# Retention and two MLPs on one core: the first in-projection of blocks 2 and 3 made wholly of seven block products

## The chip, the cores and the metric

The kernel runs on one core of a Trainium2 chip. The metric is the time of one execution on the device, in microseconds; of several runs the median is taken. A profile is one further execution, recorded instruction by instruction.

## What is computed

Three layers follow one another on 3072 tokens (4 batches of 768), all in float32:

```python
for t in range(S):                       # 8 heads of 64
    state = gamma * state + einsum('bhd,bhe->bhde', k[:, :, t], v[:, :, t])
    y[:, :, t] = scale * einsum('bhd,bhde->bhe', q[:, :, t], state)
x = y as (3072, 512)

h = np.maximum(x @ w_in, 0.0)            # w_in 512 x 2048
x = h * h @ w_out                        # w_out 2048 x 512

xn = x / sqrt(mean(x * x) + 1e-6) * rms_g
g = xn @ w_gate                          # 512 x 1536
out = (g * sigmoid(g) * (xn @ w_val)) @ w_out
```

The change is in the first product of the first MLP, `x @ w_in`.

## The kernel before, in words

**Precision.** TensorE multiplies numbers that were split in two: a high part (a cast to `fp32r`, on ScalarE) and a low part (value minus high part, on VectorE, line 102). One product of two float32 matrices is three matmuls: high x high, high x low, low x high (`mm3`, lines 281 to 283; `proj`, line 323). So every operand, weight or activation, costs a cast on ScalarE and a subtraction on VectorE before TensorE can read it. `split` does both.

**Tiling.** Tokens are cut into six blocks of 512. The first MLP's hidden width of 2048 is cut into 16 slices f of 128. Blocks 0 and 1 go through `block1`, slice by slice: 12 matmuls of `proj` make a slice of `x @ w_in`, `act1` squares it on ScalarE and casts the high half of s, VectorE makes the low half, and `out1` (12 matmuls, called by `tail1`) adds the slice's part of the second product, one slice behind. The low half of s is read first by the second matmul of `out1`.

Blocks 2 and 3 are taken as a pair, and so are 4 and 5. For a pair the in-projection can be done in four groups n of four slices, each by seven block products in place of eight (`in_pair`): the weights of a group are made into seven *in-units* (P1 to P7, sums and differences of quarters), the activations of the pair into seven operands `X[P1]` to `X[P7]`, and each of the seven products is 2 halves m x 2 halves c x 3 = 12 matmuls of 128x512. The second product of the pair is done in the same way from *out-units* (class `Out`). Units are stored in HBM as they are made (`made_units`, five steps M1 to M5 of one or two VectorE operations of 128x512 each, ahead of them one or two steps that gather rows, `whole_rows`), and are fetched through a ring of seven slots of 512 KB, from which every product takes one; `unit_done` then asks for the one seven products on.

For the first group of blocks 2 and 3 the kernel before does not use seven products. `in_phase` does slices 0 to 3 classically: 4 slices x 2 blocks x `proj`, 96 matmuls. Groups 1 to 3 use `in_pair`.

**Other work that is woven in.** The retention is computed in chunks of 128 tokens; each *visit* is some hundred small matmuls, a mask on VectorE (lines 985 and 990), a state update, and the loads of later chunks' queries, keys and values. A query must land and be decayed on GpSimd (line 944) before the next visit's scores (line 967) can use it. In block 1 there is a visit behind the projection of every even slice; in the pair's phase there are two per group, behind P6 and P3. `tick` converts one 128-row slice of a later layer's weights. `first_x` makes the operands X of blocks 2 and 3 from their retention outputs, in steps.

**Order.** The program's order is written out by hand, and each engine and each DMA queue keeps it. Python generators are advanced at fixed places by `next(...)`: `made` (out-units), `made_in` (in-units), `coming_xs` (`first_x`). In `block1` the order in a slice f is: `early(f)`, background work, projection, `act1` on ScalarE, `late(f)`, the visit with its mask if f is even, VectorE's low half of s, the visit's follow-up, `last_of(f)`, and `tail1`, which is `out1(f - 1)`. `out1(15)` itself is issued in the next phase, behind that phase's first 12 matmuls. For block 1 the hooks are `early1`, `late1` and `last1`.

Of the kernel before, what the change touches and what calls it, by code (L numbers as in the profile page):

```python
# [1 line left out]

# [47 lines left out]
NCL = 2  # L50
RING_AT = 13
# [9 lines left out]
def retention_then_two_mlps(  # L61
# [63 lines left out]
    W = {}  # L125
# [325 lines left out]
    def in_phase(xs, w_of, after, between):  # L451
        for f in range(2 * NCL):
            q, r, i = f // 4, f % 4 // 2, f % 2
            w = w_of(f)
            for t in range(2):
                proj(w, xs[t], ph[t])
                between(f, t)
                if i == 0:
                    act[r][t][q] = slot(f"act{r}{t}")
                a = act[r][t][q][:, i, :]  # L460
                nc.scalar.activation(a, ph[t], AF.Relu)
                nc.scalar.activation(a, a, AF.Square)
                after(f, t)

# [141 lines left out]
    def first_x(raws, xs):  # L606
        y = {(h, t): raws[t].t[:, 2 * h:2 * h + 2, :] for h in range(2) for t in range(2)}

        def put(src, wide=False):
            if wide:  # L610
                t = big("xop", F32R)
                o = [t[:, 0:2], t[:, 2:4]]
            else:
                o = [slot("xop", F32R) for _ in range(2)]
            split(*o, src, nc.vector)
            return o

        yield
        X[P1] = put(y[0, 0])
        yield  # L620
        X[P2] = put(y[1, 0])
        yield
        other = put(y[0, 1])
        X[P3] = put(y[1, 1])
        for a in ((X[P1], X[P2]), (other, X[P3])):
            xs.append([[a[k // 2][n][:, k % 2, :] for k in range(KC)] for n in range(2)])
        yield
        sub(y[0, 0], y[0, 1], y[0, 0])
        yield
        sub(y[0, 1], y[1, 1], y[0, 1])  # L630
        yield
        sub(y[1, 1], y[1, 1], y[0, 0])
        yield
        X[P6] = put(y[1, 1])
        yield
        X[P5] = put(y[0, 0])
        yield
        sub(y[1, 0], y[1, 0], y[1, 1])
        yield
        X[P7] = put(y[0, 1], True)  # L640
        yield
        X[P4] = put(y[1, 0], True)
        yield
# [242 lines left out]
    with tc.manual_schedule():  # L886
# [432 lines left out]
        def in_units():  # L1319
            for q in (1, 2, 3, 0):  # L1320
                yield from whole_rows("i", q)
                spare = cf.tile([128, 512], F32, tag="f", name="sm")
                for n, _ in enumerate(made_units(ui, q, row_tiles.pop(("i", q)), lambda: spare, True)):
                    if n == 1:
                        request("i", q + 1)
                    yield

        xs, raws1 = [], []
# [3 lines left out]
        def sink1(c):  # L1332
            nonlocal coming_xs
            t = c // B - 2
            if t == len(raws1):
                raws1.append(Raw())
                if t:
                    coming_xs = first_x(raws1, xs)
                    next(coming_xs)
            return raws1[t]  # L1340

        def early1(f):
            if f % 2:
                next(made, None)

        def late1(f):
# [4 lines left out]
            if f % 2:  # L1351
                next(made, None)
# [5 lines left out]

        stream += [ui[q][k] for q in range(NCL // 2, NQ) for k in IN_ORDER]

        def last1(f):
# [3 lines left out]
            next(made, None)  # L1365
# [4 lines left out]
            if f >= 4:  # L1370
                next(made_in, None)
            if f in (10, 12, 14):
                next(coming_xs)

        block1(1, cur, sink1, (0, 2, 4, 6, 8, 10, 12, 14), early1, late1, last1)
        for _ in made:
            pass
        stores()

# [25 lines left out]
        def between1(f, t):  # L1405
            if f == 0 and t == 0:
                tail1()
            else:
                background()
            mask()  # L1410

# [6 lines left out]
        def after1(f, t):  # L1418
            if t == 0:
                stores()  # L1420
                if f:
                    tick(ahead=False)
                if f and f % 2 == 0:
                    next_chunk()
            elif f % 2:
                kv, _ = visit(at_chunk, pa, True)
                after_visit(at_chunk, sink2(at_chunk), kv)
            if t or f > 1:
                next(coming_xs, None)
            if f % 2 == 0 or t == 0:  # L1430
                next(made_in, None)
            if (t or f) and len(ring) < 7:
                more_ring()

        def after1b(n, k):
            background()
            mask()
            stores()
            at_step = k in (P2, P5, P4) or k == P1 and NCL // 2 < n < NQ - 1
            if at_step:  # L1440
                tick(ahead=False)
            if (n, k) == (NCL // 2, P1) or k == P5 or k == P4 and n < NQ - 1:
                next_chunk()
# [3 lines left out]
            if at_step:  # L1447
                next(made_in, None)
            if n == NCL // 2 and k in (P2, P6, P5):
                next(coming_xs, None)  # L1450
# [16 lines left out]
        for _ in made_in:  # L1467
# [309 lines left out]
```

## Time and profile before

| | us |
|---|---|
| median of 3 runs | 1083.77 |
| lowest and highest run | 1083.15, 1086.19 |
| the profiled execution | 1085.07 |
| its span, first to last instruction | 1083.3 |

The span is what the trace covers; the execution's own time is 1.8 us longer. TensorE is called PE in the rows, its weight loads PEld, VectorE DVE, ScalarE ACT, GpSimd POOL, SyncE's queue of DMA issues SPq. L102 is line 102 of the kernel. Times in rows are microseconds from the span's start. In this execution block 1 ends, and the phase of blocks 2 and 3 begins, at 229 us; the classical first quarter lasts to 259.3 us.

### The profile page before, as it was taken

What the parts mean: (1) busy time and instruction counts of PE and PEld (TensorE: products, weight loads), DVE (VectorE), ACT (ScalarE), POOL (GpSimd) and SP (SyncE); (2) the same over time, 40 slices, a digit from 0 to 9 for tenths busy, and PEclk for the clock granted to TensorE, in tenths of its full rate; (3) what the DMA queues carried; (4) which work ended last, traced back from release to release, by engine and by line L of the source; (5) the groups of instructions that cost most, each with busy time, mean ns of one, the idle gap of its engine ahead of it and who ended that gap; (6) DMA issues with size and microseconds to landing.
All of it is one profiled execution on the core that took longest, in us unless ns stands there. A gap on an engine that the chain in (4) does not pass through costs nothing. (4 is left out here: it accounts for less than half of the span.)

```text
span 1083.3 us, 16663 instructions
## 1 busy us (share of the span) xinstructions
PE 1077.3 (99%) x6269; PEld 886.5 (82%) x6269; DVE 785.9 (73%) x1073; ACT 592.9 (55%) x915; POOL 77.2 (7%) x65
## 2 busy tenths in 40 slices
PE   9999999999999999999999999999999999999998
PEld 7788888888888887888888887888888888888887
DVE  6888689978757995579788887994343896433585
ACT  5766445767777658885465555453333554233442
POOL 3000142315210000000000000000000000000000
PEclk9999999999999999999999999999999999999999
DMA  9979889999999979987569979767567667555563
GB/s 361 337 240 353 268 283 359 380 366 357 366 367 339 344 267 394 366 279 241 199 229 338 375 274 380 256 208 241 194 231 250 193 213 251 193 194 193 194 214 117
DMA packets 109172, 303.49 MB, mean 280 GB/s; under 512 B 11124, under 2 KB 34444, under 8 KB 109092
## 3 DMA queue, kind: packets, MB, share of 16 engines
q1 hardware_dynamic: 108912, 302.18, 78.6%
q8 instruction: 50, 0.82, 0.3%
q10 hardware_dynamic: 180, 0.24, 0.1%
q14 instruction: 30, 0.25, 0.1%
HBM read 213.76 MB, written 88.62 MB: 279 GB/s over the span
## 5 line engine op out<-in xcount | busy, mean ns | idle before, releaser
L502 ACT CAST o<-act 128x1024 fp32r<-128x1024 f32 x101 | 105.5, 1051 | 110.0 <-DVE act L109 50.2
L102 DVE TENSOR_TENSOR o<-act,o 128x1024 fp32r<-128x1024 f32 x101 | 123.0, 1223 | 26.6 <-ACT o L502 26.5
L282 PE MATMUL ph<-o,ring 128*128 128x512 f32 x228 | 88.8, 389 | 0.0
L283 PE MATMUL ph<-o,ring 128*128 128x512 f32 x228 | 88.6, 388 | 0.0
L281 PE MATMUL ph<-o,ring 128*128 128x512 f32 x228 | 88.5, 388 | 0.0
L281 PE MATMUL pb<-xop,ring 128*128 128x512 f32 x208 | 81.3, 391 | 0.0
L323 PE MATMUL ph<-xh,w_i 128*128 128x512 f32 x248 | 81.1, 390 | 0.0
L283 PE MATMUL pb<-xop,ring 128*128 128x512 f32 x208 | 80.9, 389 | 0.0
L282 PE MATMUL pb<-xop,ring 128*128 128x512 f32 x208 | 80.9, 389 | 0.0
L281 PE MATMUL pa<-xop,ring 128*128 128x512 f32 x200 | 78.3, 391 | 0.3 <-ACT act L116 0.3
L109 DVE TENSOR_TENSOR act<-act 128x1024 f32<-128x1024 f32 x64 | 78.2, 1222 | 0.3
L283 PE MATMUL pa<-xop,ring 128*128 128x512 f32 x200 | 77.8, 389 | 0.0
L282 PE MATMUL pa<-xop,ring 128*128 128x512 f32 x200 | 77.8, 389 | 0.0
L281 PE MATMUL ph<-xop,ring 128*128 128x512 f32 x192 | 75.3, 392 | 0.8 <-ACT part L116 0.6
L283 PE MATMUL ph<-xop,ring 128*128 128x512 f32 x192 | 74.7, 389 | 0.0
L282 PE MATMUL ph<-xop,ring 128*128 128x512 f32 x192 | 74.7, 389 | 0.0
L112 DVE TENSOR_TENSOR part<-pr,part 128x512 f32<-128x512 f32 x38 | 25.7, 690 | 52.5 <-ACT part L116 51.2
L780 ACT ACTIVATE t<-part 128x512 f32<-128x512 f32 x54 | 34.1, 632 | 49.5 <-DVE part L112 49.5
L116 ACT COPY part<-ph 128x512 f32<-128x512 f32 x52 | 29.7, 587 | 52.3 <-PE ph L283 52.3
L323 PEld LDWEIGHTS ph<-xh,w_i 128*128 128x128 f32 x248 | 46.5, 188 | 10.2 <-ACT w_o L136 0.4
L282 PEld LDWEIGHTS ph<-o,ring 128*128 128x128 f32 x228 | 42.8, 188 | 9.7 <-DVE o L102 0.9
L281 PEld LDWEIGHTS ph<-o,ring 128*128 128x128 f32 x228 | 42.8, 188 | 9.0
(256 smaller groups left out, 2625.2 us busy)
## 6 DMA issues: line engine op xcount, KB each, us to landing
ring<-wu SPq DMA_DIRECT2D x84, 512.0 KB, 4.3
ring<-up SPq DMA_DIRECT2D x63, 512.0 KB, 4.3
ring<-uo SPq DMA_DIRECT2D x56, 512.0 KB, 4.4
ring<-ui SPq DMA_DIRECT2D x49, 512.0 KB, 7.6
wu<-ring SPq DMA_DIRECT2D x42, 512.0 KB, 6.8
raw<-w1i SPq DMA_DIRECT2D x16, 512.0 KB, 6.9
raw<-w1o SPq DMA_DIRECT2D x16, 512.0 KB, 7.0
vkt<-vk SPq DMA_DIRECT2D x16, 512.0 KB, 7.0
```

Source lines behind the costliest of these rows:

```text
L102: eng.tensor_tensor(out=dst_l, in0=src, in1=dst_h.bitcast(F32), op=ALU.subtract)
L109: eng.tensor_tensor(out=out_, in0=a, in1=b, op=ALU.subtract)
L112: eng.tensor_tensor(out=out_, in0=a, in1=b, op=ALU.add)
L116: nc.scalar.copy(dst[:, m], acc[m])
L281: nc.tensor.matmul(acc, ah, bh, start=start, stop=False, **more)
L282: nc.tensor.matmul(acc, ah, bl, start=False, stop=False, **more)
L283: nc.tensor.matmul(acc, al, bh, start=False, stop=stop, **more)
L323: nc.tensor.matmul(h, w[:, a, k * 128:(k + 1) * 128], x[b][k], start=n == 0, stop=n == len(order) - 1)
L502: nc.scalar.copy(h, src)
L780: nc.scalar.activation(t, g, AF.Silu)
```

## The change

All four groups of the in-projection of blocks 2 and 3 are done by `in_pair`; `in_phase` and its hooks are gone. For that the in-units of group 0 are needed at the start of the phase and not for blocks 4 and 5 only, so `in_units` goes through the groups in the order 0, 1, 2, 3, begins two slices earlier in block 1 and is advanced more often there; the out-units are advanced less often in block 1, and what is left of them (`making_1`) follows in the phase of blocks 2 and 3. The ring is filled from slice 10 on (`RING_AT`) and not from 13. `first_x` makes no second set of plain operands (`other`) any more, and has three differences and the operand P6 ready by the end of block 1; P5, P7 and P4 follow behind the first three products of group 0.

```diff
-NCL = 2
-RING_AT = 13
+RING_AT = 10
...
-    def first_x(raws, xs):
+    def first_x(raws):
...
-        other = put(y[0, 1])
-        X[P3] = put(y[1, 1])
-        for a in ((X[P1], X[P2]), (other, X[P3])):
-            xs.append([[a[k // 2][n][:, k % 2, :] for k in range(KC)] for n in range(2)])
+        put(P3, y[1, 1])
         yield
         sub(y[0, 0], y[0, 1], y[0, 0])
-        yield
         sub(y[0, 1], y[1, 1], y[0, 1])
         yield
         sub(y[1, 1], y[1, 1], y[0, 0])
         yield
-        X[P6] = put(y[1, 1])
-        yield
-        X[P5] = put(y[0, 0])
+        put(P6, y[1, 1])
+        yield
+        put(P5, y[0, 0])
+        yield
+        put(P7, y[0, 1], True)
         yield
         sub(y[1, 0], y[1, 0], y[1, 1])
...
-            for q in (1, 2, 3, 0):
+            for q in range(NQ):
                 yield from whole_rows("i", q)
...
         def early1(f):
-            if f % 2:
-                next(made, None)
+            if f % 2 and f != 11:
+                next(made)
+            if f == NF1 - 1:
+                next(coming_xs)
 
         def late1(f):
...
-            if f % 2:
-                next(made, None)
+            if f == NF1 - 1:
+                next(coming_xs)
+            if f % 2 and f > 1:
+                next(made_in)
+            elif f % 2:
+                next(made)
...
-        stream += [ui[q][k] for q in range(NCL // 2, NQ) for k in IN_ORDER]
+        stream += [ui[q][k] for q in range(NQ) for k in IN_ORDER]
 
         def last1(f):
             stores()
             if f >= RING_AT:
                 more_ring()
-            next(made, None)
+            if f < 8 or f % 2 == 0 and f != 10:
+                next(made)
             if f == MORE_AT:
                 more_steps(W2_SOON)
             if f > MORE_AT and f % 2:
                 tick(ahead=False)
-            if f >= 4:
+            if f >= 2:
                 next(made_in, None)
-            if f in (10, 12, 14):
+            if f in (8, 10, 14, 15):
                 next(coming_xs)
...
-        for _ in made:
-            pass
         stores()
+        making_1 = chain(made_in, made)
...
+        def after1(n, k):
+            if (n, k) == (0, P1):
+                tail1()
+            else:
+                background()
             mask()
             stores()
-            at_step = k in (P2, P5, P4) or k == P1 and NCL // 2 < n < NQ - 1
+            at_step = k in (P2, P5, P4) or k == P1 and 0 < n < NQ - 1
             if at_step:
                 tick(ahead=False)
-            if (n, k) == (NCL // 2, P1) or k == P5 or k == P4 and n < NQ - 1:
+            if k == P5 or k == P4 and n < NQ - 1:
                 next_chunk()
             if k in (P6, P3):
                 kv, _ = visit(at_chunk, (ph, pb)[(n + 1) % 2] if k == P6 else pa, True)
                 after_visit(at_chunk, sink2(at_chunk), kv)
             if at_step:
-                next(made_in, None)
-            if n == NCL // 2 and k in (P2, P6, P5):
-                next(coming_xs, None)
+                next(making_1, None)
+            if n == 0 and k in (P1, P2, P6):
+                next(coming_xs)
+            if (n, k) == (0, P1):
+                more_ring()
...
-        in_phase(xs, lambda f: W[("i", f)], after1, between1)
-        for n in range(NCL // 2, NQ):
-            in_pair(n, after1b)
+        for n in range(NQ):
+            in_pair(n, after1)
```

## Rows read from the trace of the kernel before

**Rows 1.** The page's totals: busy us, share of the span, instructions

```profile
PE 1077.3 (99%) x6269; PEld 886.5 (82%) x6269; DVE 785.9 (73%) x1073; ACT 592.9 (55%) x915; POOL 77.2 (7%) x65
```

**Rows 2.** TensorE's waits: who for whom, us in total, times, longest

```profile
PE pr L1095 <- DVE st L1080: 1.3, 1, 1.3
PE ph L281 <- ACT part L116: 0.6, 2, 0.4
PE pa L281 <- ACT act L116: 0.3, 1, 0.3
```

**Rows 3.** Line 323 from 229 us on: duration ns min/median/max, first and last start

```profile
L323 PE MATMUL ph<-xop,w_i x96: 388/389/499, 229.0 to 256.3; 128*128 128x512 f32 x96
```

**Rows 4.** Timeline of TensorE across block 1's end: start us, duration, instruction

```profile
229.02 2.88 PE L323 MATMUL ph<-xop,w_i 128*128 128x512 f32 x12
231.74 0.39 PE L281 MATMUL pa<-s,w_o 128*128 128x512 f32 x1
231.97 0.39 PE L282 MATMUL pa<-s,w_o 128*128 128x512 f32 x1
```

**Rows 5.** Timeline of VectorE, slices 14 and 15; in brackets idle time and releaser

```profile
220.87 0.43 DVE L985 TENSOR_TENSOR causal<-ph,seen_sb 128x256 f32<-128x256 f32 x1 [1.04 <-PE ph L967]
...
223.84 0.69 DVE L109 TENSOR_TENSOR sm<-sm,rows 128x512 f32<-128x512 f32 x1
224.44 1.10 DVE L102 TENSOR_TENSOR made<-rows,made 128x512 fp32r<-128x512 f32 x1
225.47 3.20 DVE L102 TENSOR_TENSOR xop<-raw,xop 128x1024 fp32r<-128x1024 f32 x2
228.59 1.78 DVE L102 TENSOR_TENSOR s<-r,s 128x512 fp32r<-128x512 f32 x1
230.29 0.68 DVE L102 TENSOR_TENSOR wps<-rows,wps 128x512 fp32r<-128x512 f32 x1
```

**Rows 6.** Timeline of VectorE in slice 13

```profile
214.75 1.22 DVE L102 TENSOR_TENSOR xop<-raw,xop 128x1024 fp32r<-128x1024 f32 x1
215.89 0.68 DVE L102 TENSOR_TENSOR made<-rows,made 128x512 fp32r<-128x512 f32 x1
```

**Rows 7.** Timeline of GpSimd beside rows 5

```profile
224.07 0.93 POOL L1033 TENSOR_TENSOR st<-st,sdec_sb 128x256 f32<-128x256 f32 x1 [9.79 <-DMA rows<-rows_i]
224.96 1.49 POOL L955 TENSOR_TENSOR vkt<-vkt,vdec_sb 128x512 f32<-128x512 f32 x1
227.91 1.91 POOL L944 TENSOR_TENSOR qnt<-qnt,qdec_sb 128x512 f32<-128x512 f32 x1 [1.46 <-DMA qnt<-qT]
```

**Rows 8.** Timeline of ScalarE, the cast of slice 15's s

```profile
227.80 0.62 ACT L339 CAST s<-r 128x512 fp32r<-128x512 f32 x1
```

**Rows 9.** Windows of two stretches (classical quarter, group 1): length, busy us (instructions), clock, DMA

```profile
229.00:259.30 30.30, 30.30 (x269) 25.04 (x267) 20.61 (x27) 21.18 (x36) 9.02 (x6) 1.00 1.00 396
259.30:282.20 22.90, 22.90 (x249) 18.68 (x241) 19.54 (x34) 15.18 (x26) 9.37 (x7) 1.00 1.00 369
```

**Rows 10.** Line 1357, the ring's first seven loads, 512 KB each

```profile
DMA to landing us min/median/max: 8.5/8.8/9.6
```

**Rows 11.** Timeline of TensorE: visits of the classical quarter, then scores of group 1's two

```profile
242.71 0.69 PE L1002 MATMUL pr<-vkt 128*64 128x64 f32 x16
...
245.47 11.18 PE L323 MATMUL ph<-xop,w_i 128*128 128x512 f32 x48
256.58 0.69 PE L1002 MATMUL pr<-vkt 128*64 128x64 f32 x16
...
270.21 0.85 PE L967 MATMUL ph<-qnt,kTt 64*64 64x128 f32 x32
...
281.37 0.85 PE L967 MATMUL pa<-qnt,kTt 64*64 64x128 f32 x32
```

**Rows 12.** Timeline of SyncE's queue: issue of the query load between these two

```profile
270.51 0.33 SPq L922 DMA_DIRECT2D qnt<-qT  x1
```

**Rows 13.** Timeline of GpSimd: decay of that query

```profile
278.06 1.30 POOL L944 TENSOR_TENSOR qnt<-qnt,qdec_sb 128x512 f32<-128x512 f32 x1 [3.79 <-DMA qnt<-qT]
```

More of the change, by code (lines that the diff above doesn't have):

```diff
@@ L1 @@
 from contextlib import ExitStack
+from itertools import chain
 import numpy as np
@@ L449, in unit_done @@
         load_unit(ring_at[0] + 6)
[L451 to L463, printed above, removed]
     class Out:
@@ L604, in raw_x, with put @@
         yield
-    def first_x(raws, xs):
+    def first_x(raws):
         y = {(h, t): raws[t].t[:, 2 * h:2 * h + 2, :] for h in range(2) for t in range(2)}
-        def put(src, wide=False):
+        def put(k, src, wide=False):
             if wide:
                 t = big("xop", F32R)
-                o = [t[:, 0:2], t[:, 2:4]]
+                X[k] = [t[:, 0:2], t[:, 2:4]]
             else:
-                o = [slot("xop", F32R) for _ in range(2)]
-            split(*o, src, nc.vector)
-            return o
+                X[k] = [slot("xop", F32R) for _ in range(2)]
+            split(*X[k], src, nc.vector)
         yield
-        X[P1] = put(y[0, 0])
+        put(P1, y[0, 0])
         yield
-        X[P2] = put(y[1, 0])
+        put(P2, y[1, 0])
         yield
-        other = put(y[0, 1])
-        X[P3] = put(y[1, 1])
-        for a in ((X[P1], X[P2]), (other, X[P3])):
-            xs.append([[a[k // 2][n][:, k % 2, :] for k in range(KC)] for n in range(2)])
+        put(P3, y[1, 1])
         yield
         sub(y[0, 0], y[0, 1], y[0, 0])
-        yield
         sub(y[0, 1], y[1, 1], y[0, 1])
@@ L633, in first_x @@
         yield
-        X[P6] = put(y[1, 1])
+        put(P6, y[1, 1])
         yield
-        X[P5] = put(y[0, 0])
+        put(P5, y[0, 0])
+        yield
+        put(P7, y[0, 1], True)
         yield
         sub(y[1, 0], y[1, 0], y[1, 1])
-        yield
-        X[P7] = put(y[0, 1], True)
-        yield
-        X[P4] = put(y[1, 0], True)
+        put(P4, y[1, 0], True)
         yield
@@ L1326, in in_units @@
                     yield
-        xs, raws1 = [], []
+        raws1 = []
         made_in = in_units()
@@ L1337, in sink1 @@
                 if t:
-                    coming_xs = first_x(raws1, xs)
+                    coming_xs = first_x(raws1)
                     next(coming_xs)
@@ L1403, in retention_then_two_mlps @@
         stream += [uo[q][k] for k, q in out_1.seq]
[L1405 to L1410, printed above, removed]
         def next_chunk():
@@ L1416, in next_chunk @@
             at_chunk += 1
[L1418 to L1428, printed above, removed]
-                next(coming_xs, None)
-            if f % 2 == 0 or t == 0:
-                next(made_in, None)
[L1432 to L1436, printed above, removed]
+        def after1(n, k):
[3 more added lines that the diff above has]
+                background()
             mask()
             stores()
-            at_step = k in (P2, P5, P4) or k == P1 and NCL // 2 < n < NQ - 1
+            at_step = k in (P2, P5, P4) or k == P1 and 0 < n < NQ - 1
             if at_step:
                 tick(ahead=False)
-            if (n, k) == (NCL // 2, P1) or k == P5 or k == P4 and n < NQ - 1:
+            if k == P5 or k == P4 and n < NQ - 1:
                 next_chunk()
@@ L1447, in after1b @@
             if at_step:
-                next(made_in, None)
-            if n == NCL // 2 and k in (P2, P6, P5):
-                next(coming_xs, None)
+                next(making_1, None)
[3 more added lines that the diff above has]
+                more_ring()
             if n == NQ - 1 and k in (P2, P6, P3):
@@ L1465, in retention_then_two_mlps @@
             background()
-        for _ in made_in:
+        for _ in making_1:
             pass
```

## The prediction

> **What bounds the kernel now.** I read the page's totals first, then TensorE's waits, then the stretch that the change rewrites, engine by engine. TensorE is busy for 99% of the span [rows 1], and its waits on other engines come to 2.2 us in the whole execution [rows 2]; the same view of 100 to 340 us alone lists none. Busy time of pipelined matmuls proves little, so I looked at their starts: twelve matmuls of the classical product take from 229.02 to 231.74 us [rows 4], 0.227 us for each, and the matmuls of the seven-product groups have the same form. So TensorE is packed: a matmul left out is worth 0.227 us, and any wait that is made for it costs its full length. What decides is whether VectorE, ScalarE, GpSimd and the DMAs, all busy in this stretch [rows 9], still deliver in time after the work has been laid out anew.
>
> **What is removed and added on TensorE.** The classical first quarter is 8 projections of 12 matmuls, the 96 of [rows 3]. The new group 0 is 7 products of 2 x 2 x 3 = 84. So 12 matmuls go: 12 x 0.227 = **-2.72 us**. Both layouts have the same eight visits of the retention, so the small matmuls and the switches between them and the large ones cancel. No other large matmul changes.
>
> **What is moved onto VectorE ahead of block 1's last out-projection.** This is where I expect the gain to go. In `block1` the program is emitted per slice f: `early`, projection, `act1`, `late`, the visit, then the low half of s (`low(s)`), then `last_of`, and each engine keeps this order. out1(15) runs on TensorE directly after the first product of the next stage (12 matmuls before and after alike). Its second matmul, at 231.97 us [rows 4], is the first that reads the low half of s(15). Before, VectorE starts that subtraction at 228.59, just behind ScalarE's cast of 227.80 + 0.62 us [rows 5, 8], and is free again at 230.29. So the slack is 231.97 - 230.29 = 1.7 us, and VectorE had come to it without a pause.
>
> What stands in front of it, counted from 223.84 us, where visit 14's own work on VectorE is over (its mask waits for TensorE until 220.87, so VectorE can't come to this earlier [rows 5]):
>
> - Before: one step of an in-unit (two operations of 128x512), the low halves of two operands (two of 128x1024), then s: 3 small and 2 large ones.
> - After: `last1(14)` emits a step of an out-unit (2 small), a step of an in-unit (2 small) and one operand's low half (1 large); `early1(15)` a step of an out-unit (2 small) and two quarter differences (2 large); `late1(15)` the third difference (1 large) and an in-unit's last step (1 small); then s: 8 small and 4 large ones.
>
> A small one takes 0.60 us from start to start (223.84 to 224.44, [rows 5]), a large one 1.14 (214.75 to 215.89, [rows 6]). Before that makes 3 x 0.60 + 2 x 1.14 = 4.08 us, but 223.84 to 230.29 is 6.45: 2.37 us more. The stretched operations (1.10, 3.20 for two, 1.78 us) are the ones that run while GpSimd has its three operations [rows 7]; these don't move, since the state update and the landed loads release them. After: 8 x 0.60 + 4 x 1.14 = 9.36, with the same 2.37 us 11.73, so s(15) is done at 223.84 + 11.73 = 235.57 us. TensorE wants it at 231.97: a wait of **+3.60 us**. Bounds: without any stretch 9.36 us, done at 233.20, wait 1.23; with all of GpSimd's 0.93 + 1.49 + 1.91 = 4.33 us paid by VectorE, done at 237.53, wait 5.56. I take 3.60, since it carries the stretch that the same three operations cost in this very place.
>
> The Trainium skill (SBUF — State Buffer, the part on ports) says that a VectorE operation with two SBUF inputs and a GpSimd operation that reads SBUF lock each other out for a whole operation, whichever starts first. The trace agrees in kind (an operation of 0.69 us takes 1.78 beside GpSimd's 1.91) and charges VectorE 2.37 of 4.33 us; if VectorE lost every turn, as the rule allows, the sum would be the upper bound above. The rule speaks against packing more onto VectorE here.
>
> **What I cost at nothing, and its cover.** Slices 12 and 13 carry as much as before (10 small operations, against 8 small and a large one, without s) and visit 14's mask has 1.04 us of idle time ahead of it [rows 5]. Slices 2 and 3 get two steps more (2.4 us), but s of an odd slice is read only after an out-projection and the next projection, 2.7 us each, and that slice's visit, about 3 us (242.71 to 245.47, [rows 11]); slice 15 is the one odd slice that no visit follows, which is why it alone is tight. In group 0 the operand P6 (ready some 2.4 us behind s(15): two tick operations and a large one, 238) is read at about 240.8 (235.57, 11 matmuls of out1(15), 12 of the product P2), P5 and P7 later still. New on ScalarE and VectorE in group 0 are the copies and additions that every group has; group 1, the same code with the last operands made in it, runs today with VectorE busy 19.5 of 22.9 us and no wait of TensorE [rows 2, 9]. The seventh ring unit is asked for five products, 13.6 us, and two visits ahead of its use, against landings of 8.5 to 9.6 us [rows 10]. The steps of out-units that slide behind block 1 feed products that come behind all four groups. If the cover of P6 were gone, another 1 to 2 us would be lost.
>
> **The sum.** -2.72 + 3.60 = +0.88 us on the profiled execution: 1085.07 + 0.88 = 1085.95. That execution is 1.30 us above the median of the runs (1083.77), so the median becomes **1084.65**, say 1084.7. With the two bounds of the wait it is 1082.3 to 1086.6. The three runs of before spread over 0.28%, so about 0.3% (3.25 us) is what a measurement can tell from no change: by this sum the two halves cancel within that.
>
> **Rivals.**
>
> *The full gain.* VectorE delivers s(15) in time, so only the 12 matmuls count: 1083.77 - 2.72 = 1081.05. For it: TensorE is packed, every matmul shows. Against it: even without any stretch by GpSimd VectorE is 1.23 us late, so it needs an order of work other than the program's. Even so it is -0.25%, on the near side of what can be told.
>
> *Slower: the DMAs of group 0.* Its place is the query load between the two visits of a group. Today in group 1 the scores start at 270.21 and, in the next visit, at 281.37; between them the query is loaded (issued at 270.51, landed for GpSimd at 278.06) and decayed for 1.30 us [rows 11 to 13]: ready at 279.36, 2.0 us ahead. In today's classical quarter the visits are 13.9 us apart (242.71 and 256.58, [rows 11]); group 0 brings the 11.2 us of group 1 into a stretch whose DMA share is already 1.00 at 396 GB/s [rows 9]. It also adds loads there: each of its products fetches a unit, about 8 loads against the 4 that take the ring from three slots to seven today, so 4 x 0.52 MB, 5.3 us at that rate. If all of it stands ahead of the query load, that takes 7.55 + 5.3 = 12.9 us and the visit waits 3.3 us: with the +0.88 a total of +4.2, 1088.0. It decides (over 0.3%) from a landing of about 12 us on. For it: share 1.00. Against it: only half of the added loads are issued before that query, 2.7 us, which leaves a wait of 0.7; and the longest landing shown there is 9.6 us [rows 10].
>
> The Trainium skill (DMA: Bandwidth & Descriptors, "Where 436 GB/s comes from") puts HBM's share of a core at about 358 GB/s and the fabric at 435; by the first figure this rival would be certain. The rows show 396 GB/s over 30 us, so the first figure doesn't bind here.
>
> *Slower or faster by small waits elsewhere.* TensorE's three short waits on copies [rows 2] could move with the phases, 0.9 us in all without the one at the start; that changes no verdict.
>
> **How the numbers follow.** The wait at out1(15), between its bounds: 0.58. Full gain, or a wait so small that most of it is left: 0.20. Slower by late DMAs on top of the wait: 0.16. The small waits and what I don't see: 0.06. Faster by over 0.3% can't come from the sum alone (2.72 < 3.25), only from the full gain with half a microsecond found elsewhere or a favourable median: 0.08. Slower by over 0.3%: the DMA rival's larger half and a wait beyond its bound: 0.14. The same: 0.78. The range runs from the full gain, 1081.0, to short of the DMA rival's full price, 1087.4.
>
> **What the profile after will show.** Right: 6257 TensorE matmuls in place of 6269; the 96 `L323` matmuls on `xop` gone; one wait of TensorE of 1.2 to 5.6 us in block 1's last out-projection, released by VectorE's s; just before it VectorE without a gap from visit 14's mask on. Wrong: no such wait and a span 2.7 us shorter, or VectorE idle ahead of s(15), which would mean that the order of its work was not as I read it; or waits of TensorE at visits, released by GpSimd's query or a DMA, which is the second rival.

## The result, and the profile after

| | us |
|---|---|
| after, median of 4 runs (lowest, highest) | 1091.09 (1090.71, 1092.07) |
| before, 4 runs beside them | 1084.07 (1083.15, 1086.19) |
| ratio after / before, 95% interval | 1.0063 [1.0046, 1.0081] |
| profiled execution of after, its span | 1091.07, 1089.4 |

The change made the kernel 0.6% slower. 1091.09 us lies 6.4 us over the predicted time and 3.7 us over the upper end of the range. The page's totals of the kernel after:

```profile
PE 1075.7 (99%) x6257; PEld 885.1 (81%) x6257; DVE 785.4 (72%) x1078; ACT 593.5 (54%) x913; POOL 74.2 (7%) x65
```

TensorE has 12 matmuls and 1.6 us of busy time less than in [rows 1], no instruction of line 323 is left from 229 us on, and yet the span is 6.1 us longer. So TensorE waited. Its waits, kernel after (who for whom, us in total, times, longest):

```profile
PE pa L282 <- DVE s L102: 3.8, 1, 3.8
PE pr L982 <- issue: 3.1, 1, 3.1
PE pr L1075 <- DVE st L1060: 1.3, 1, 1.3
PE ph L281 <- ACT part L116: 0.6, 1, 0.6
PE pa L947 <- POOL qnt L924: 0.6, 1, 0.6
...
```

The third and the fourth stand in [rows 2] too (with line numbers 20 higher for the third). New are the first, which is the predicted one, the second, which is not, and the fifth, which is the rival of the query loads in small.

**The predicted wait.** Timeline of TensorE in block 1's last out-projection, kernel after:

```profile
231.57 0.39 PE L281 MATMUL pa<-s,w_o 128*128 128x512 f32 x1
235.78 0.80 PE L282 MATMUL pa<-s,w_o 128*128 128x512 f32 x1 [3.82 <-DVE s L102]
236.37 0.63 PE L283 MATMUL pa<-s,w_o 128*128 128x512 f32 x1
...
239.03 0.40 PE L281 MATMUL pb<-s,w_o 128*128 128x512 f32 x1
```

The second matmul, due 0.227 us behind the first, starts 4.21 us behind it: 3.98 us lost, where the sum had 3.60. Timeline of VectorE ahead of it, kernel after:

```profile
220.70 0.43 DVE L965 TENSOR_TENSOR causal<-ph,seen_sb 128x256 f32<-128x256 f32 x1 [0.97 <-PE ph L947]
...
223.67 0.69 DVE L109 TENSOR_TENSOR sm<-sm,rows 128x512 f32<-128x512 f32 x1
224.27 1.10 DVE L102 TENSOR_TENSOR made<-rows,made 128x512 fp32r<-128x512 f32 x1
225.30 1.53 DVE L109 TENSOR_TENSOR rows<-rows,sm 128x512 f32<-128x512 f32 x1
226.75 1.77 DVE L102 TENSOR_TENSOR made<-sm,made 128x512 fp32r<-128x512 f32 x1
228.44 1.21 DVE L102 TENSOR_TENSOR xop<-raw,xop 128x1024 fp32r<-128x1024 f32 x1
...
230.78 3.73 DVE L109 TENSOR_TENSOR raw<-raw 128x1024 f32<-128x1024 f32 x3
234.44 0.68 DVE L102 TENSOR_TENSOR made<-rows,made 128x512 fp32r<-128x512 f32 x1
235.04 0.68 DVE L102 TENSOR_TENSOR s<-r,s 128x512 fp32r<-128x512 f32 x1
```

There is no bracket behind the mask: VectorE is never idle, it is late. The three stretched operations run from 224.27 to 228.44, 4.17 us for what takes 1.80 unhindered: 2.37 us, the very figure of before. This is the row that bears on the port rule of the Trainium skill (SBUF — State Buffer, "SBUF: two separate sides"), by which one of the two engines blocks for whole operations: VectorE again pays a bit over half of GpSimd's 4.15 us (0.93 + 1.49 + 1.73). But these 4.15 us hold GpSimd's own waiting: elsewhere in this trace the same three operations take 0.61, 1.04 and 1.26 us (at 261.49, 250.64 and 257.82), 2.91 in all. Of these VectorE paid 2.37, so the trace is nearer to the rule than the 4.15 let it seem. The three differences take 1.22 us from start to start and not 1.14, 0.24 more.

**The clock behind it.** Windows of the kernel after: length, busy us of TensorE, weight loads, VectorE, ScalarE, GpSimd (instructions), granted clock, DMA share, GB/s:

```profile
229.00:231.50 2.50, 2.50 (x13) 2.07 (x12) 2.50 (x4) 1.43 (x3) 0.00 (x0) 1.00 1.03 421
231.80:235.70 3.90, 0.15 (x1) 0.00 (x0) 3.83 (x6) 1.15 (x2) 0.00 (x0) 0.94 0.53 217
235.70:238.80 3.10, 3.02 (x8) 2.40 (x9) 2.85 (x5) 1.46 (x3) 0.00 (x0) 0.53 0.98 274
```

After the wait the granted clock is 0.53, the lower level (1.2 GHz of 2.4) for nearly the whole window. From 235.78 to 239.26 nine matmuls start in 3.48 us; at 0.227 each it would be 2.04. That is 1.44 us more which the sum did not hold.

**The second wait.** It is at group 1's first visit, behind P6. Line 982 there multiplies keys and values into the bank `pr`, where P2's product lay; VectorE must first have added that product to its sums (`act<-pr`, line 112). In the kernel before, the timeline of VectorE there is:

```profile
265.31 1.29 DVE L112 TENSOR_TENSOR act<-pr,act 128x512 f32<-128x512 f32 x2
266.52 0.68 DVE L246 SCALAR_TENSOR_TENSOR f<-f,raw 128x512 int32<-128x512 int32 x1
```

And that of TensorE:

```profile
267.72 0.69 PE L1002 MATMUL pr<-vkt 128*64 128x64 f32 x16
```

The addition is over at 266.52 and wanted at 267.72: 1.2 us to spare. Timeline of VectorE at the same place, kernel after:

```profile
268.46 0.98 DVE L246 SCALAR_TENSOR_TENSOR f<-f,raw 128x512 int32<-128x512 int32 x1 [0.71 <-ACT raw L235]
269.37 1.78 DVE L109 TENSOR_TENSOR rows<-rows,sm 128x512 f32<-128x512 f32 x1
271.07 1.76 DVE L102 TENSOR_TENSOR made<-sm,made 128x512 fp32r<-128x512 f32 x1
272.87 1.29 DVE L112 TENSOR_TENSOR act<-pr,act 128x512 f32<-128x512 f32 x2
```

Timeline of TensorE there, kernel after:

```profile
270.76 0.39 PE L283 MATMUL pb<-xop,ring 128*128 128x512 f32 x1
274.26 0.69 PE L982 MATMUL pr<-vkt 128*64 128x64 f32 x16 [3.11 <-issue]
```

Timeline of GpSimd in groups 0 and 1, kernel after:

```profile
257.82 1.26 POOL L924 TENSOR_TENSOR qnt<-qnt,qdec_sb 128x512 f32<-128x512 f32 x1 [6.14 <-DMA qnt<-qT]
...
267.36 1.53 POOL L924 TENSOR_TENSOR qnt<-qnt,qdec_sb 128x512 f32<-128x512 f32 x1 [3.00 <-DMA qnt<-qT]
268.86 3.43 POOL L418 TENSOR_TENSOR y<-y 128x512 f32<-128x512 f32 x2
```

P2's matmuls are over by 268.5, but three operations now stand ahead of the addition on VectorE: a conversion (`tick`) and a unit's step, 4.4 us from 268.46 to 272.87. They are there because the diff's condition `0 < n < NQ - 1` gives group 1 a step behind P1, which before only group 2 had. The step's two operations are stretched from 0.6 to 1.7 and 1.8 us by GpSimd's additions for the norm (line 418), which queued behind the decay of a query that landed late. The view of waits says "issue" here, so it shows no releaser; the place of the addition, which ends at 274.16, just ahead of the matmuls that start at 274.26, does. 274.26 - 270.76 is 3.50 us, of which 0.32 us is the usual step from a product to a visit in this phase: 3.18 us lost.

**The sum of the parts, in the profiled execution.** -2.72 (12 matmuls) + 3.98 + 1.44 + 3.18 + 0.6 (the query in group 0's second visit) = +6.5 us; the spans differ by 6.1.

### The profile page after: what moved, and what is told of

The parts are those of the page before. It is cut to its first block, busy times and chain, and to the rows that moved or that the text cites. A ratio compares the mean times of both kernels' runs of the same rounds, so it can differ in the third digit from the quotient of the medians.

```text
span 1089.4 us, 16634 instructions
## 1 busy us (share of the span) xinstructions
PE 1075.7 (99%) x6257; PEld 885.1 (81%) x6257; DVE 785.4 (72%) x1078; ACT 593.5 (54%) x913; POOL 74.2 (7%) x65
## 5 line engine op out<-in xcount | busy, mean ns | idle before, releaser
L109 DVE TENSOR_TENSOR act<-act 128x1024 f32<-128x1024 f32 x68 | 83.0, 1220 | 0.3
L281 PE MATMUL ph<-xop,ring 128*128 128x512 f32 x208 | 81.4, 391 | 0.6 <-ACT part L116 0.6
L281 PE MATMUL pa<-xop,ring 128*128 128x512 f32 x208 | 81.4, 391 | 0.0
L282 PE MATMUL ph<-xop,ring 128*128 128x512 f32 x208 | 81.0, 389 | 0.0
L283 PE MATMUL ph<-xop,ring 128*128 128x512 f32 x208 | 81.0, 389 | 0.0
L283 PE MATMUL pa<-xop,ring 128*128 128x512 f32 x208 | 80.9, 389 | 0.0
L282 PE MATMUL pa<-xop,ring 128*128 128x512 f32 x208 | 80.9, 389 | 0.0
```

Of the source, the lines that this page charges most:

```text
L109: eng.tensor_tensor(out=out_, in0=a, in1=b, op=ALU.subtract)
L281: nc.tensor.matmul(acc, ah, bh, start=start, stop=False, **more)
L282: nc.tensor.matmul(acc, ah, bl, start=False, stop=False, **more)
L283: nc.tensor.matmul(acc, al, bh, start=False, stop=stop, **more)
```

## The experiments

Each kernel is compared with the kernel before on the same chip; the ratios have 95% intervals. "Listed" is the sum of TensorE's waits in the profile (2.2 us before, 9.8 after).

| kernel | median us | before beside it | ratio | listed us |
|---|---|---|---|---|
| no_step_in_group1 | 1088.14 | 1083.53 | 1.0042 [1.0028, 1.0055] | 5.8 |
| late_differences | 1091.35 | 1083.53 | 1.0068 [1.0053, 1.0083] | 10.5 |
| later_norm_sums | 1092.36 | 1083.53 | 1.0076 [1.0058, 1.0095] | 9.9 |
| before_plus_4 | 1090.91 | 1083.53 | 1.0065 [1.0050, 1.0080] | 7.3 |
| before_spare_3 | 1086.51 | 1083.60 | 1.0028 [1.0019, 1.0037] | 4.9 |
| before_spare_5 | 1090.39 | 1083.60 | 1.0064 [1.0050, 1.0078] | 6.3 |
| light_slice15 | 1089.43 | 1083.60 | 1.0056 [1.0042, 1.0070] | 8.5 |
| light_with_step | 1091.16 | 1083.60 | 1.0069 [1.0055, 1.0083] | 8.1 |
| paced | 1085.88 | 1083.62 | 1.0023 [1.0011, 1.0034] | 7.0 |
| paced_queries_first | 1086.18 | 1083.62 | 1.0022 [1.0013, 1.0030] | 5.4 |
| paced_more_steps | 1086.61 | 1083.34 | 1.0031 [1.0021, 1.0041] | 6.0 |
| paced_more_steps_queries_first | 1087.35 | 1083.34 | 1.0036 [1.0023, 1.0049] | 5.1 |

### The step that the condition put into group 1

On the kernel after:

```diff
-            at_step = k in (P2, P5, P4) or k == P1 and 0 < n < NQ - 1
+            at_step = k in (P2, P5, P4) or k == P1 and 1 < n < NQ - 1
```

> The changed kernel without the conversion step and the unit step behind group 1's product P1 (groups 2 and 3 keep their places; the unit steps all move one place on). Theory A (the wait of 3.2 us at group 1's first visit is for VectorE's addition of product P2, which stands behind that step): the wait goes, 1091.1 - 3.2 = 1087.9 us; the wait at s(15) and the low clock behind it stay. Rival (a query or value load is late): the visit goes on waiting some 3 us, 1091.

1088.14 us: as expected to 0.3. VectorE's addition in the timeline of this kernel:

```profile
267.57 1.45 DVE L112 TENSOR_TENSOR act<-pr,act 128x512 f32<-128x512 f32 x2
```

And the first of TensorE's waits in it:

```profile
PE pa L282 <- DVE s L102: 3.8, 1, 3.8
```

The addition is over at 269.0, well ahead of the visit's first matmul (270.88); GpSimd's additions run here too, for 2.66 us from 268.66 on, but by then it is nearly done. The waits of the visit and of the query are gone, that for s(15) and the clock behind it have stayed. With one condition undone, 2.95 us of the loss go away by the medians (1091.09 - 1088.14), or 2.4 when each is taken against the kernel before beside it (7.0 and 4.6 us). This settles the mechanism of the second wait.

### GpSimd's part in that wait

On the kernel after, the norm's squares (ScalarE) and additions (GpSimd) come later:

```diff
-                back.append(norm1(pj, 2 + 2 * pj))
+                back.append(norm1(pj, 2 + 8 * pj))
```

> The changed kernel with GpSimd's three additions for block 1's norm moved six products later, so that they no longer run beside group 1's unit step; the step itself stays. Theory A (VectorE's step there took 3.5 us and not 1.2 because of GpSimd's additions, which had waited behind a query's decay): the wait at group 1's first visit falls from 3.2 to about 0.5 us, 1091.1 - 2.7 = about 1088.4 us. Rival (the step alone is what delays the addition, GpSimd plays no part): the wait falls by less than 1 us.

1092.36 us, a miss in the time and right in the wait. Waits of TensorE in this kernel:

```profile
PE pr L359 <- DVE act L112: 1.5, 1, 1.5
...
PE pr L982 <- issue: 0.9, 1, 0.9
```

And one of its windows, behind s(15), with the columns as above:

```profile
235.70:242.60 6.90, 5.72 (x14) 4.47 (x15) 4.78 (x8) 4.46 (x7) 0.00 (x0) 0.51 0.82 233
```

The wait at group 1's first visit falls from 3.1 to 0.9 us, so 2.2 us of it go with these additions. The rest is the added step, and in part GpSimd once more: one operation ahead of the step, at 268.82, takes 1.78 us beside the decay of a query. But the additions now meet a later visit, where TensorE waits 1.5 us, and the wait for s(15), just as long as before (4.22 us between the two starts), is followed by the lower clock for 6.8 us in place of 3.4: 13 matmuls start in 5.70 us in place of 2.95, some 2.8 us lost.

### The three differences out of the way of s(15)

On the kernel after, the differences and P6 are made behind s(15) in slice 15 and not ahead of it:

```diff
-            if f == NF1 - 1:
-                next(coming_xs)
...
-            if f == NF1 - 1:
-                next(coming_xs)
...
+            if f == NF1 - 1:
+                for _ in range(3):
+                    next(coming_xs)
...
-            if f in (8, 10, 14, 15):
+            if f in (8, 10, 14):
```

> The changed kernel, but the three differences of the operands (three VectorE operations of 128x1024) and P6 are made behind the low half of s(15) and not ahead of it. Theory A (the wait of 4.0 us in block 1's last out-projection is VectorE's queue ahead of s(15), and the slow matmuls behind it are the clock that fell during that wait): three operations take 3 x 1.14 to 3.66 us, so the wait shrinks from 3.8 to about 0.3 us and the clock stays at its upper level, worth 1.4 us more. But the same VectorE work then stands ahead of the addition of product P2, so I expect a new wait of about 2 us at group 0's first visit: 1091.1 - 3.6 - 1.4 + 2.3 = about 1088.4 us. Rival (a load or a stored unit is late in that place, not VectorE): the wait stays at 3.8 us, and the time at 1091.

1091.35 us: the time of after, a miss; the new wait at group 0's first visit came as expected. Waits of TensorE in this kernel:

```profile
PE pr L982 <- issue: 5.0, 2, 3.1
PE pa L947 <- POOL qnt L924: 1.6, 1, 1.6
...
PE ph L281 <- ACT act L116: 1.3, 1, 1.3
...
PE pa L282 <- DVE s L102: 0.2, 1, 0.2
```

The wait for s(15) has gone from 3.8 to 0.2 us, so the differences were what made it. Their 3.7 us on VectorE have not: P6 is late, ScalarE, which casts it (236.06, idle for 6.99 us until the differences are there), comes late to the copies of the first product, and TensorE waits 1.3 us for those, 1.9 us at group 0's first visit and 1.0 us more for a query. The lower clock has moved too, from behind s(15) to the wait at group 1 (0.51 from 273.4 to 276.9). What one place gained, three others gave back, and the fall of the clock only changed its place.

### The loss at s(15) on the kernel before

If VectorE's lateness alone makes the first wait, it can be made on the kernel before, which has neither the new group nor its loads. Spare operations of 128x1024 in slice 15 write a tile that nothing reads; they add work and change no result.

```diff
+            if f == NF1 - 1:
+                spare = slot('spare', F32R)
+                for _ in range(3):
+                    low(nc.vector, spare, raws1[0].t[:, 0:2, :], X[P1][0])
```

> The kernel before with three VectorE operations of 128x1024 ahead of slice 15's projection, written to a spare tile that nothing reads. Theory A: 3 x 1.14 = 3.4 us against 1.7 us of slack: TensorE waits about 1.7 us in block 1's last out-projection, and after so short a wait the clock stays up: 1083.5 + 1.7 = 1085.2 us. Rival (VectorE's queue is not what s(15) waits for): 1083.5 us.

1086.51 us, 1.3 above what was expected. Windows of this kernel:

```profile
231.30:234.10 2.80, 0.84 (x4) 0.39 (x3) 2.77 (x4) 0.00 (x0) 0.00 (x0) 1.00 1.02 418
234.10:237.50 3.40, 3.40 (x10) 2.63 (x9) 2.53 (x5) 0.92 (x2) 0.00 (x0) 0.50 1.05 404
```

TensorE's second matmul of out1(15) starts 2.12 us late (233.68), and in this execution the clock falls behind even this wait: from 233.68 to 237.88 eleven matmuls take 4.20 us in place of 2.50. It does not do so each time. Of the ten runs five have a mean granted clock of 0.998, as this one, and a median of 1087.0 us; the other five have 1.000 and a median of 1085.7, close to the expected time. With five spare operations:

> The same with five operations: 5 x 1.14 = 5.7 us against 1.7 us of slack, a wait of 4.0 us as in the changed kernel. Theory A with the clock: the granted clock falls to its lower level behind that wait and costs 1.4 us (one stretch of 3.4 us) to 2.8 us (two): 1083.5 + 4.0 + 1.4 to 2.8 = 1088.9 to 1090.3 us. Rival (the slow matmuls belong to the new group's transfers, not to the wait): full clock, 1087.5 us.

1090.39 us, at the upper end of what was expected. TensorE's first wait in it:

```profile
PE pa L282 <- DVE s L102: 4.5, 1, 4.5
```

And its window behind the wait:

```profile
234.50:241.30 6.80, 5.94 (x14) 4.70 (x15) 4.60 (x8) 2.67 (x5) 0.00 (x0) 0.50 0.74 283
```

The kernel before, with VectorE loaded like this, is as slow as the kernel after. So the first wait and the slow matmuls behind it belong to VectorE's queue and to the wait, not to the new group or its transfers. A first form of this test repeated the low half of the operand P1 itself:

```diff
+            if f == NF1 - 1:
+                for _ in range(4):
+                    low(nc.vector, X[P1][1], raws1[0].t[:, 0:2, :], X[P1][0])
```

> The kernel before with four VectorE operations of 128x1024 put ahead of slice 15's projection, each a repetition of one that was done already (same inputs, same result), so that nothing else changes. Theory A: VectorE had 1.7 us of slack in front of s(15); four operations of 1.14 us are 4.6 us, so TensorE waits 2.9 us in block 1's last out-projection, and at that length the clock may still stay at its upper level: 1084.1 + 2.9 = 1087.0 us, or 1088.4 with a fall of the clock as in the changed kernel. Rival (VectorE's queue is not what s(15) waits for): 1084.

1090.91 us, a miss by its layout: the next stage's first product reads P1's low half in its second matmul, so TensorE waited there, 5.3 us from 229.11 on and ahead of out1(15), for the last writer of the tile. It says how much 4 operations cost at another place, and nothing of s(15).

### Both waits taken away at once

On the kernel after, slice 15's unit steps and conversion are left to the groups, no step stands behind P1 of group 1, and a unit's step stands behind P7 of groups 1 to 3 instead:

```diff
-            if f % 2 and f != 11:
+            if f % 2 and f not in (11, 15):
                 next(made)
...
-            if f % 2 and f > 1:
+            if f % 2 and 1 < f < 15:
                 next(made_in)
...
-            if f < 8 or f % 2 == 0 and f != 10:
+            if f < 8 or f in (8, 12):
...
-            if f > MORE_AT and f % 2:
+            if f > MORE_AT and f % 2 and f < 15:
                 tick(ahead=False)
-            if f >= 2:
+            if 2 <= f < 14:
                 next(made_in, None)
...
-            at_step = k in (P2, P5, P4) or k == P1 and 0 < n < NQ - 1
+            at_step = k in (P2, P5, P4) or k == P1 and 1 < n < NQ - 1
...
-            if at_step:
+            if at_step or k == P7 and n:
                 next(making_1, None)
```

> The changed kernel with less VectorE work between visit 14 and group 0's first visit: the unit steps of slices 14 and 15 (two of out-units, three of in-units) and slice 15's conversion step are left to the groups (a unit step more behind P7 of groups 1 to 3), the differences stay where they were; and no step behind group 1's P1. Theory A: s(15) is ready by about 231.5 us, so no wait or one under 0.5 us in block 1's last out-projection, no fall of the clock, no wait at group 1's visit; what is left is the 12 matmuls less 2.7 us and a query's wait of up to 1 us: 1083.5 - 2.7 + 0.5 = 1081.3 us, a ratio of about 0.998. Rival (the loads that group 0 adds are the real limit and come to light once VectorE is out of the way): waits of 2 us and more at the visits of groups 0 to 2, 1083 to 1086 us.

1089.43 us, a miss by 8. In the profiled execution both waits are gone and the clock stays at 1.00. Waits of TensorE that have come in their place:

```profile
PE pa L947 <- POOL qnt L924: 1.7, 1, 1.7
PE pa L282 <- DVE ol L102: 1.7, 1, 1.7
...
```

The query of group 2's second visit is issued late on SyncE's queue (295.12), behind a store that waits for a unit's low half; the out-projection's operands are late, since one conversion more has slid into that stage (the one at 349.18 waits 2.17 us for ScalarE). The same kernel with the step behind P1 of group 1 put back (`0 < n`):

> The same with the step behind group 1's P1 put back (a conversion and a unit step ahead of the addition of P2). Theory A, if the two waits are independent: a wait of 1 to 3.5 us at group 1's first visit comes back and none at s(15): 1082.5 to 1085 us. Rival (that wait was an after-effect of the delay at s(15)): no wait, 1081.3 us as without the step.

1091.16 us: right in the wait, a miss by 6 in the time. Its wait at group 1's first visit:

```profile
PE pr L982 <- issue: 3.2, 1, 3.2
```

It is back without any wait for s(15), so it does not need that wait. That it has its old length is chance, for its make-up is another. The step is a different one here, and GpSimd doesn't stretch its two operations (0.71 and 0.69 us); VectorE is idle ahead of it, for a tile that a store of converted weights still reads:

```profile
266.08 0.71 DVE L112 TENSOR_TENSOR sm<-rows 128x512 f32<-128x512 f32 x1 [2.33 <-DMA wq<-f]
```

### Spread further

As light_slice15, but slice 15 keeps its conversion, no group has a step behind P1, and unit steps stand behind every P7 and behind P3 of group 1:

```diff
-            if f > MORE_AT and f % 2 and f < 15:
+            if f > MORE_AT and f % 2:
...
-            at_step = k in (P2, P5, P4) or k == P1 and 1 < n < NQ - 1
+            at_step = k in (P2, P5, P4)
...
-            if at_step or k == P7 and n:
+            if at_step or k == P7 or (n, k) == (1, P3):
```

> Seven products for all four groups, with the unit steps of slices 14 and 15 left to the groups as in light_slice15, but slice 15's conversion step kept, no step at all behind any group's P1 (so nothing stands ahead of the addition of P2), and a unit step behind P7 of every group and behind P3 of group 1. Theory A (VectorE's order is the cause of the larger waits; those of the out-projection in light_slice15 came from conversions that ran on into it): no wait at s(15), none at a first visit of a group, none of the out-projection's operands; the queries may still be 0 to 2 us late at one or two visits, since their loads stand behind stores in SyncE's queue: 1083.6 - 2.7 + 1 to 2 = 1082 to 1083 us. Rival (the eighth saved needs transfers that this stretch doesn't have): 1085 us and more.

1085.88 us: the lowest median of all forms with seven products everywhere, and still 0.2% slower than before. The expected 1082 to 1083 us are missed, and the time is the one that its rival was given, by which this stretch lacks the transfers. From out1(15) to the end of group 3 no listed wait of TensorE is longer than 0.3 us. The longest wait stands much later, at 454.24 (1.4 us for a copy by ScalarE), and ahead of it ScalarE's timeline in this kernel has a wait of its own:

```profile
446.75 0.66 ACT L232 ACTIVATE rows<-raw 128x512 f32<-128x512 f32 x1 [4.51 <-DMA raw<-w2o]
```

The last two conversions of weights come some 3.4 us later there than in the kernel before (446.75 and 450.42, against 443.26 and 447.08). The listed waits have grown by 7.0 - 2.2 = 4.8 us, which with -2.72 makes +2.1, against +2.3 by the medians. But 1.1 us of these waits are for loads in the first 40 us, and they come without the change too: before_spare_3, whose edit stands in slice 15 of block 1 alone, has 1.6 us of them, above all this one:

```profile
PE ph L967 <- DMA stage<-qk: 1.4, 1, 1.4
```

Without them the waits make +1.0, and 1.3 us of the loss are not accounted for.

If late query loads were the rest, stores put behind the visit's loads should help:

```diff
-            stores()
+            if k not in (P6, P3):
+                stores()
...
             if k in (P6, P3):
...
+                stores()
```

> The same with the stores of finished units issued behind a visit's loads, not ahead of them. Theory A: a query that was late because SyncE's queue waited for a unit's low half is now on time; waits at visits under 0.5 us in all, so nearly the whole gain of the 12 matmuls shows: 1081 to 1081.8 us, ratio 0.998. Rival (the queries are late because the DMA engines are full, not because of their place in the queue): waits as in paced, same time.

1086.18 us, the time of paced: a miss. The queries are in time, but now the scores of group 1's second visit wait 1.2 us; the view gives no releaser, and by its place it is VectorE's addition out of the bank that they write. And if what slides into later stages is the rest, more conversions in the groups (behind P7 of groups 1 to 3) should help:

```diff
-            if at_step:
+            if at_step or k == P7 and n:
                 tick(ahead=False)
```

> paced with a conversion step more behind P7 of groups 1 to 3, so that the conversions are three places ahead and not one behind when the out-projection begins. Theory A (what paced still loses, some 3 us behind the first in-projection, are conversions and loads that slid into the out-projection and the pair of blocks 4 and 5): the waits there fall back to those of the kernel before and the time to 1083 us or less. Rival (VectorE and ScalarE have no room in groups 1 to 3 either): new waits at the visits of groups 1 to 3, 1086 us or more.

1086.61 us, no gain on paced and the time of the rival. The wait at 454 and those on the out-projection's operands are gone or under 0.3 us. But in group 1 this kernel's timeline of VectorE reads:

```profile
278.10 0.69 DVE L246 SCALAR_TENSOR_TENSOR f<-f,raw 128x512 int32<-128x512 int32 x1 [2.45 <-ACT raw L235]
278.72 0.67 DVE L109 TENSOR_TENSOR rows<-rows,sm 128x512 f32<-128x512 f32 x1
279.32 0.67 DVE L102 TENSOR_TENSOR made<-sm,made 128x512 fp32r<-128x512 f32 x1
279.93 1.27 DVE L112 TENSOR_TENSOR act<-pa,act 128x512 f32<-128x512 f32 x2
```

And its window from the wait's end on:

```profile
281.00:284.40 3.40, 3.25 (x35) 2.74 (x35) 3.27 (x9) 0.66 (x2) 2.06 (x2) 0.50 0.98 379
```

VectorE is idle for 2.45 us, not busy: the conversion waits for ScalarE, which has waited 4.06 us until the store of an earlier conversion had freed its tile, and the addition of P3 stands behind it in VectorE's order. TensorE waits 2.2 us at 280.70 for that addition, and the lower clock follows. ScalarE's timeline in this kernel:

```profile
276.82 0.68 ACT L232 ACTIVATE f<-raw 128x512 f32<-128x512 f32 x1 [4.06 <-DMA wq<-f]
```

With both edits:

> The same with the stores of finished units behind a visit's loads. Theory A: at most the same time, 1082 to 1083 us. Rival: as for paced_more_steps, 1086 us or more.

1087.35 us, 4 above what was expected, with a wait of 2.6 us at the same place. No version here beats the kernel before; paced and paced_queries_first come nearest, and their intervals lie wholly on the slower side.

## Why the prediction was wrong

**Right: the gain.** 12 matmuls went, 0.227 us each, with no other large matmul changed: 6257 matmuls, TensorE 1.6 us less busy though seven of them took longer than they would have.

**Right: the wait for s(15).** Its place, its releaser, VectorE without idle time, and the stretch by GpSimd (2.37 us) are those of the prediction. That the stretch agrees to the hundredth is partly luck, since other operations were stretched and GpSimd's third one started 1.67 us earlier. 3.98 us in place of 3.60: VectorE began 0.17 us earlier than in [rows 5], its differences took 0.24 us more than assumed, TensorE came to the place 0.17 us earlier than in [rows 4], and it went on at 235.78, 0.14 us behind the 235.64 at which the sum's way of counting ends s(15). The upper bound of 5.56 us was set too high: the 4.33 us of GpSimd's that it charges to VectorE hold GpSimd's own waiting. late_differences shows that the differences make this wait.

**Wrong: "What I cost at nothing, and its cover".** The step that failed is this sentence's: "group 1, the same code with the last operands made in it, runs today with VectorE busy 19.5 of 22.9 us and no wait of TensorE". It is not the same code. The condition of `at_step` in the diff moves `tick` and a unit's step ahead of the addition of P2, and the 3.4 us that VectorE was idle in [rows 9] are an average over the group which is of no use to an operation that stands behind another one. The two traces give the price: 4.4 us put in front of an addition that had 1.2 us to spare is 3.2, and 3.18 was measured. That it fits so well is partly luck, for in no_step_in_group1 the same addition has 1.86 us to spare (269.02 against 270.88), and with the step it ends 3.08 us behind the visit's due time, 4.9 us later. no_step_in_group1 shows that the condition is the cause; later_norm_sums that 2.2 us of it go with GpSimd's additions. Without any stretch the move would have cost 0.6 us from rows of before (conversion and step, 3 x 0.60, against 1.2). No rival had this wait: the sign given for waits at visits was a release by GpSimd's query or a DMA, and here it is VectorE.

**Wrong: the clock.** The sum charged a wait at its own length. Here it was followed by matmuls at the lower clock, 1.44 us more; before_spare_3 (in five of its ten runs) and before_spare_5 show that it belongs to the wait, since the kernel before pays it too.

**The rival of the query loads.** Right in kind, and small: the query of group 0's second visit, issued at 247.55, landed for GpSimd at 257.82, 10.3 us later, and TensorE waited 0.6 us, near the 0.7 of the milder case. The windows show 421 GB/s at the phase's start, so the 358 GB/s of the Trainium skill (DMA: Bandwidth & Descriptors, "Where 436 GB/s comes from") did not bind here either. For the kernel after, the two waits and the clock leave the DMAs a small part of the sum, though they have a hand in the second wait: GpSimd's additions stood behind a decay that had waited 3.00 us for its query. For the spread forms they are not cleared. Reordering the queue changed nothing (paced and paced_queries_first), which speaks only against the order of the loads; and ScalarE waits 4.51 us for a load in paced and 4.06 us for a store in paced_more_steps, VectorE 2.33 us for a store in light_with_step, and the DMAs are busy throughout there (share 1.03 in paced from 250 to 270 us, 1.01 from 425 to 447). That the seven products lack transfers there was not tried by itself.

**Why the forms tried here don't mend it.** The work of VectorE and ScalarE stays what it was (785.4 and 593.5 us busy, against 785.9 and 592.9). Slice 15, the groups and the stages behind them were each tried as its place, and at each the loss came back, as another wait: 1.3 to 1.9 us in group 0 (late_differences), 1.7 us on the out-projection's operands (light_slice15), 1.4 us in the phase of blocks 4 and 5 (paced), 2.2 us in group 1 (paced_more_steps). What is spread best has 4.8 us more of listed waits, 3.7 of them behind the first 40 us, for 2.72 us of matmuls.

**Open.** The profiled executions differ from the medians by up to 1.5 us, and the runs of paced scatter from 1083.17 to 1089.39. A part of that is the clock: its two longest runs (1089.21 and 1089.39) have a mean granted clock of 0.998, the other ten 0.999 or 1.000. Which of its small waits stand in every execution is not known, nor what makes the 1.3 us that its waits leave over. In light_slice15 the listed waits and the 12 matmuls make +3.6 of the +5.8 us by the medians.

## What to carry to other kernels

When a diff moves work on an engine that runs in order, find, for each place that it is moved to, the next operation behind it that the bound engine waits for, and read that one's slack in time; the engine's idle share over the stage doesn't answer it. Read every changed condition as a move, with the loop values that it newly lets in. Price a wait of TensorE of 2 us or more with the matmuls behind it at half clock as well: here 1.4 to 2.8 us where it came, and it did not come in every execution. And a saving of 2.7 us on an engine that is 99% busy is worth having only if the others have that much slack at the places where it makes them earlier.

## What the runs showed of the hardware that was not expected

In the middle of a kernel that had run at a granted clock of 1.00 from its start, one pause of TensorE could be followed by the lower level: after 2.1 us of pause for 3.4 us (before_spare_3), after 4.0 us for 3.4 (after) or 6.8 us (later_norm_sums, the same pause of 4.22 us between two starts), after 4.6 us for 6.8 (before_spare_5). At that level matmuls of 128x512 start 0.427 us apart and not 0.227. The length of the pause does not decide alone: the 3.2 us at group 1's first visit cost no clock in the kernel after (1.00 in the 7 us behind it) and did in late_differences (0.51 from 273.4 to 276.9) and light_with_step (0.59 from 268.2 to 271.6). Nor is it the same in every execution of one kernel: before_spare_3 has a mean clock of 0.998 in five runs and 1.000 in five, 1.3 us apart by their medians, and the kernel after 0.998 in two runs and 0.995 in two. So the price of one and the same wait differs by up to 2.8 us between versions of a kernel, and differs between runs of one, which makes small rearrangements look better or worse than their waits.
